# K turned in 32 by 32 squares on VectorE instead of on TensorE, in a decode block of cached attention and a gated MLP

## The chip, the cores and the metric

The kernel runs on one core of one Trainium2 chip. The metric is the device time of one execution in microseconds. A profiled execution also gives a span, which is about 1.8 us shorter than its time. Runs are called fast or slow: here a run is slow when it lies over 1.5% above the fastest run of the same kernel. All ratios use fast runs.

Engine names in the profile: PE is TensorE, PEld its weight loads, DVE is VectorE, ACT is ScalarE, POOL is GpSimd, SP issues the DMAs. PEclk is the clock that TensorE was granted; in the text, *warm* is the full clock and *cold* is half of it: the profile's windows over one PV of the changed kernel show a granted clock of 1.00 where its products took 1.90 us and of 0.50 where they took 3.59.

## The reference, cut to what matters

```python
# x: 1x1x640; 32 heads of 128; caches 1x32x4096x128; MLP 640 -> 1728 -> 640; all bf16
h  = x + A(layernorm(x))            # A: one query against 4096 cached keys and values, then wo
q  = (x @ wq).reshape(..., 32, 128)
p  = softmax(einsum("bhqd,bhkd->bhqk", q, k_cache) * 128 ** -0.5)
A  = einsum("bhqk,bhkd->bhqd", p, v_cache).reshape(..., 4096) @ wo
h2 = h + (gelu(hn @ w_gate) * (hn @ w_up)) @ w_down      # hn = layernorm(h)
```

Each cached key and value is used once. The two caches are 67 MB of the 84 MB that the kernel reads.

## The kernel before

Four heads are one *quad*. A quad's K is one tile of 128 partitions by 128 rows by 128 columns (4 MB); its V has the same shape. The score products of this kernel contract over partitions, so K has to be turned before them. The kernel before does this with 128 products per quad against an identity matrix; VectorE and ScalarE copy the turned K from PSUM back to SBUF. K and V have two buffers each.

```python
def pe_transposes(slot, mark, after):
    ...
    for g in range(NG):                       # 16 groups of 8 products of 128 x 128
        ...
        for b in range(GRP):
            inst = PE.transpose(tp_b[g % NBANK][:, b * DH : (b + 1) * DH], kt[slot][:, g * GRP + b, :], ident[:])
...
def pe_scores(slot, half, ready, mark):       # 128 products with 4 columns
    ...
        inst = PE.matmul(s_ps[half][:, j % (NB // 2), :], lhsT=kt[slot][:, j, :],
                         rhs=q8[:, slot * QH : (slot + 1) * QH], start=True, stop=True)
...
def pe_pv(slot, half, mark):                  # 128 products with 4 columns
    ...
        inst = PE.matmul(o_ps, lhsT=vt[slot][:, j, :], rhs=e_t[:, j, :], start=(j == 0), stop=(j == NB - 1))
...
with nc.Fori(0, TURNS, engines=(only_pe,), head_slot={only_pe: HEAD}):   # two quads a turn
...
for m in range(NQ):                           # the order of the loads, on one queue
    load_k(m)                                 # waits for the scores of quad m-2; the last K in two halves
    if m in (0, 2, 4):
        load_wo(m // 2)
    ...
    load_v(m)                                 # waits for PV of quad m-2
load_wo(TURNS - 1)
load("wg", ...); load("wu", ...)              # then the four pieces of w_down
```

The softmax here doesn't subtract the row's maximum and nothing guards it: scores larger than these inputs give would overflow.

Of the kernel before, what the change touches and what calls it, by code (L numbers as in the profile page):

```python
# [9 lines left out]
def kernel(  # L10
# [13 lines left out]
    nc = tc.nc  # L24
    bf16 = mybir.dt.bfloat16
# [18 lines left out]
    GRP = 8  # L44
    NG = NB // GRP
    YR = 4
    YW = D // YR
    TURNS = NQ // SLOTS
    HG = QH * SLOTS
    NBANK = 4  # L50
    HEAD = 0
    ON_ACT = (1, 4, 6, 9, 11, 14)
# [22 lines left out]
    big = sb("big", [P, 2 * SLOTS * TILE + 2 * W_MLP], bf16)  # L75
# [4 lines left out]
    def tile_at(i):  # L80
        return part(i * TILE, TILE).rearrange("p (j d) -> p j d", d=DH)

    kt = [tile_at(i) for i in range(SLOTS)]
    vt = [tile_at(SLOTS + i) for i in range(SLOTS)]
    wq_sb = part((2 * SLOTS - 1) * TILE, DC * NH * DH).rearrange("p (c n) -> p c n", c=DC)
    wg_sb = part(2 * SLOTS * TILE, W_MLP).rearrange("p (c f) -> p c f", c=DC)
    wu_sb = part(2 * SLOTS * TILE + W_MLP, W_MLP).rearrange("p (c f) -> p c f", c=DC)
# [14 lines left out]
    q_row = sb("q_row", [P, 2, 4 * DH], bf16)  # L102
    q_sb = sb("q_sb", [P, NH], bf16)
    q8 = sb("q8", [P, HG], bf16)
    e_t = sb("ex", [P, NB, QH], bf16)
    rs_all = sb("rs_all", [P, 2, NH])
    rs_cur = sb("rs_cur", [P, HG])
    rinv = sb("rinv", [P, HG])
    o_raw = sb("o_raw", [P, NH])
# [24 lines left out]
    tp = [bank(f"tp{i}") for i in range(NBANK)]  # L134
    tp_b = [t.bitcast(bf16) for t in tp]
    tp_g = [t[:].rearrange("p (b d) -> p b d", d=DH) for t in tp_b]
    s_bank = [bank(f"s{h}") for h in "ab"]
    o_bank, a_bank = bank("o"), bank("a")
    s_ps = [t[:, 0 : QH * NB // 2].rearrange("p (j i) -> p j i", i=QH) for t in s_bank]
    attn_ps = a_bank[:, 0:YW]  # L140
    qr_ps = s_bank
    q_ps = tp_b[0]
    o_ps = o_bank[:, 0:QH]

    def small(b):
        return b[:, 16 : 16 + 2 * DC], b[:, 32 : 32 + HG], b[:, 48 : 48 + HG]

    (m_ps, t_ps, r_ps), (m_end, t_end, r_end) = small(o_bank), small(tp[3])
    g_ps, u_ps, y_ps = tp[0][:, 0 : RG + LAST], tp[1][:, 0 : RG + LAST], tp[2][:, 0:YW]

    names = (
        [f"{t}{i}{h}" for t in "kv" for i in range(SLOTS) for h in "ab"]
        + ["x", "wq", "wo", "wo_in", "wg", "wu", "wd0", "wd1", "wd2", "wd3", "out"]
        + ["pe", "dve", "act", "pool", "q", "dve_pe", "act_pe", "y", "all"]
# [39 lines left out]
    for ps in (attn_ps, qr_ps[0][:], qr_ps[1][:]):  # L194
        dve(lambda: DVE.memset(ps, 0.0), False)
    dve(lambda: DVE.memset(rs_all[:], 0.0), False)
    DVE_RS = dve(lambda: DVE.memset(rs_cur[:], 1.0), False)
    dve(lambda: DVE.memset(ones_f[:], 1.0), False)
    POOL_IDENT, POOL_E, POOL_COPIED = 2, 3, 6
    DVE.wait_ge(S["pool"], POOL_IDENT)  # L200
    by_c = ident[:].rearrange("p (c j) -> p c j", j=HG)
    with nc.allow_low_precision(reason="sums of one 1 and zeros"):
        dve(lambda: DVE.reduce_sum(row_of[:], by_c, AX.X), False)
        dve(lambda: DVE.reduce_sum(col_of[:], by_c.rearrange("p c j -> p j c"), AX.X), False)

# [33 lines left out]
    DVE_Q = DVE_XN + 2  # L239

    def group(slot, g):
        return kt[slot][:, g * GRP : (g + 1) * GRP, :]

    def pe_transposes(slot, mark, after):
        ready = [("act_pe", EA_T[slot][g]) if g in ON_ACT else ("dve_pe", EV_T[slot][g]) for g in range(NG)]
        for g in range(NG):
            if g % (NG // 2) == 0:
                landed(f"k{slot}{'ab'[g // (NG // 2)]}")
            if g >= NBANK:
                PE.wait_ge(S[ready[g - NBANK][0]], ready[g - NBANK][1])  # L250
            for b in range(GRP):
                inst = PE.transpose(  # L252
                    tp_b[g % NBANK][:, b * DH : (b + 1) * DH], kt[slot][:, g * GRP + b, :], ident[:]
                )
            mark(("T", g), inst)
            if g in after:
                after[g]()
        return ready[-NBANK:]

    def pe_scores(slot, half, ready, mark):  # L260
        for j in range(half * NB // 2, (half + 1) * NB // 2):
            g, b = divmod(j, GRP)
            if b == 0 and g >= NG - NBANK:
                PE.wait_ge(S[ready[g - NG + NBANK][0]], ready[g - NG + NBANK][1])
            inst = PE.matmul(  # L265
                s_ps[half][:, j % (NB // 2), :],
                lhsT=kt[slot][:, j, :],
                rhs=q8[:, slot * QH : (slot + 1) * QH],
                start=True,
                stop=True,  # L270
            )
        mark(("s", half), inst)

    def pe_pv(slot, half, mark):
        landed(f"v{slot}{'ab'[half]}")
        PE.wait_ge(S["act_pe"], EA_EXP[slot][half])
        for j in range(half * NB // 2, (half + 1) * NB // 2):
            inst = PE.matmul(  # L278
                o_ps, lhsT=vt[slot][:, j, :], rhs=e_t[:, j, :], start=(j == 0), stop=(j == NB - 1)
            )  # L280
            if j == NB // 2:
                mark("pv first", inst)
        mark("pv", inst)

    def pe_project(w, mark, last):
        for j in range(HG):
            for r in range(YR):
                inst = PE.matmul(  # L288
                    attn_ps[32 * r : 32 * r + 1, :],
                    lhsT=o_row[:, j : j + 1],  # L290
                    rhs=w[:, j, r * YW : (r + 1) * YW],
                    start=False,
                    stop=last and j == HG - 1,
                    skip_group_check=True,
                    tile_position=(0, 32 * r),
                )
        mark("project", inst)
# [21 lines left out]
    ON_DVE = [g for g in range(NG) if g not in ON_ACT]  # L319
    SPREAD_AT, ROW_AT = 3, 6  # L320
    EV_Q, EV_RS = 1, 3
    EV_T = [{}, {}]
    n = EV_RS
    for i, g in enumerate(ON_DVE):
        if i == SPREAD_AT:
            n += 1
            EV_SPREAD = n
        if i == ROW_AT:
            n += 1
            EV_ROW = n  # L330
        n += 1
        EV_T[0][g] = n
    n += 1
    for g in ON_DVE:
        n += 1
        EV_T[1][g] = n
    EV_ALL = n
    EA_T, EA_EXP = [{}, {}], [[], []]
    n = 0
    for slot in range(SLOTS):  # L340
        for g in ON_ACT:
            n += 1
            EA_T[slot][g] = n
        EA_EXP[slot] = [n + 1, n + 2]
        n += 2
    EA_ALL = n

    start = mark_at("start")
    PE.wait_ge(S["dve"], DVE_XS)
    pe_moments(m_ps, x_col, start)  # L350

    def pe_queries():
        PE.wait_ge(S["dve"], DVE_XN)
        for c in range(DC):
            if c == 0:
                landed_once("wq")
            for b in range(2):
                for r in range(4):
                    h = 16 * b + 4 * r
# [3 lines left out]
                        rhs=wq_sb[:, c, h * DH : (h + 4) * DH],  # L363
# [6 lines left out]
        PE.wait_ge(S["pool"], POOL_IDENT)  # L370
        PE.wait_ge(S["act"], 1)
        PE.wait_ge(S["dve"], DVE_Q - 1)
        for b in range(2):
            for i in range(4):
                k = (4 * b + i) * P
                inst = PE.transpose(q_ps[:, k : k + P], q_row[:, b, i * DH : (i + 1) * DH], ident[:])
        inst.then_inc(S["q"], 1)

    pe_queries()
    PE.wait_ge(S["dve"], DVE_Q)  # L380
    PE.wait_ge(S["pool"], POOL_COPIED)

    base = done["pe"]
    only_pe = mybir.EngineType.PE
    with nc.Fori(0, TURNS, engines=(only_pe,), head_slot={only_pe: HEAD}):
        for slot in range(SLOTS):
            mark = mark_at(slot)
            after = {}
            if slot == 0:

                def totals():
                    PE.wait_ge(S["dve_pe"], EV_RS)
                    pe_totals(t_ps, mark)

                def reorder():
                    PE.wait_ge(S["dve_pe"], EV_SPREAD)
                    pe_reorder(r_ps, mark)

                after = {ON_DVE[SPREAD_AT - 1]: totals, 8: reorder}
            ready = pe_transposes(slot, mark, after)  # L400
            if slot == 0:
                PE.wait_ge(S["dve_pe"], EV_ROW)
                PE.wait_ge(S["wo"], 1)
                PE.sem_inc(S["wo"], -1)
                pe_project(wo_t, mark, False)
            for half in range(2):
                pe_scores(slot, half, ready, mark)
            for half in range(2):
                pe_pv(slot, half, mark)
        PE.sem_inc(S["dve_pe"], -EV_ALL)  # L410
        PE.sem_inc(S["act_pe"], -EA_ALL)
# [95 lines left out]
    def load_kv(which, m, tiles, src, free):  # L507
        slot = m % SLOTS
        if m >= SLOTS:
            SP.wait_ge(S["pe"], free)  # L510
# [216 lines left out]
```

## Time and profile before

| | before |
|---|---|
| time, median of 6 runs | 206.97 us (206.08 to 207.66) |
| span of the profiled run | 204.8 us |
| busy: PE, DVE, ACT | 145.5, 73.4, 81.4 us |
| DMA | 84.4 MB, share 0.99 to 1.01 from 20 to 180 us |
| first product of the MLP | 192.72 us |

The page of the kernel before. The first lines give busy time, share of the span and instructions of each engine; the other two are the DMA's busy share and rate in 40 equal slices, where a 9 is 90% or more.

```profile
...
PE 145.5 (71%) x3409; PEld 135.7 (66%) x3409; DVE 73.4 (36%) x185; ACT 81.4 (40%) x179; POOL 19.2 (9%) x17
...
DMA  7999999999999999999999999999999999999990
GB/s 248 408 458 416 396 475 406 437 432 451 406 419 416 441 426 448 435 429 410 435 448 398 447 455 416 422 435 448 429 429 416 416 429 461 429 401 432 400 350 32
...
```

No engine is busy all the time, but the DMA is, from the second slice to the last but one. The windows of the same run say it with numbers; the last three columns are the granted clock, the DMA's share and its rate.

```profile
...
100.00:120.00 20.00, 16.44 (x388) 16.21 (x386) 7.64 (x17) 9.92 (x22) 0.00 (x0) 0.74 1.00 429
...
199.00:201.00 2.00, 1.60 (x44) 1.09 (x48) 0.22 (x2) 0.00 (x0) 0.00 (x0) 0.50 0.43 163
201.00:203.00 2.00, 0.76 (x20) 0.31 (x20) 0.33 (x2) 0.00 (x0) 0.00 (x0) 0.50 0.00 0
...
```

The DMA ends in the window from 199 to 201 us. What is left after it is a short tail. Two lines of the chain of waits (start, duration, what; the span is that of the profiled run) mark the last quad: the first of its products with the identity, and the product that follows its PV.

```profile
...
170.75 0.87 PE tp_103 L252 x8
...
187.15 0.54 PE tp_106 L300 x2
...
```

The last quad's K is turned from 170.75 on, and its PV product ends at 187.15. The timeline of TensorE shows the rest. The columns are start, duration, engine, line, operation, output and inputs, number, and in brackets the idle time before it and what ended that.

```profile
...
192.72 2.16 PE L454 MATMUL tp_103<-big,hc 128*1 128x416 bf16 x25 [0.53 <-DVE hc L664]
196.09 2.16 PE L454 MATMUL tp_104<-big,hc 128*1 128x416 bf16 x25 [1.22 <-DMA big<-in_B_w_up_dram]
199.40 2.36 PE L437 MATMUL tp_105<-big,hid 128*1 128x160 bf16 x60 [1.15 <-DVE hid L680]
```

The MLP begins at 192.72. The up product (196.09) waits for its weights from the DMA, and the down product (199.40) takes 2.36 us. It waits for `hid`, which VectorE writes from both products:

```profile
...
199.07 0.18 DVE L680 TENSOR_TENSOR hid<-g_sb,u_col 128x15 bf16<-128x15 f32 x1
...
```

### The profile page before, as it was taken

To read this page: it belongs to the slowest core of one execution; us is meant where nothing else is said; L and a number is where in the kernel's file an instruction comes from. 1 tells how busy PE (TensorE), PEld (TensorE's weight loads), DVE (VectorE), ACT (ScalarE), POOL (GpSimd) and SP (SyncE) were. 2 spreads that over 40 slices of the span, in tenths; PEclk is the share of its full clock that TensorE was granted. 3 is DMA by queue.
4 is the path that set the end of the run, shared out by engine and by line. 5 is a ranking of instruction groups with operands and counts; after the bars stand their busy time and mean duration, and the time that the engine had idled before them with its cause. 6 is when DMAs were issued, how large, how long until landed. Compare 5 with 4: busy or idle time off the path is not lost. (4 is left out here: it accounts for less than half of the span.)

```text
span 204.8 us, 7384 instructions
## 1 busy us (share of the span) xinstructions
PE 145.5 (71%) x3409; PEld 135.7 (66%) x3409; DVE 73.4 (36%) x185; ACT 81.4 (40%) x179; POOL 19.2 (9%) x17
## 2 busy tenths in 40 slices
PE   0001769935997399849984998299839989986654
PEld 0000269935997399849974997299739979986322
DVE  4006126500570058005701660047006702832570
ACT  0000234533377047704670557037704671771000
POOL 8300000340000001700000026000000000000000
PEclk9999967975797579757975797579757975995555
DMA  7999999999999999999999999999999999999990
GB/s 248 408 458 416 396 475 406 437 432 451 406 419 416 441 426 448 435 429 410 435 448 398 447 455 416 422 435 448 429 429 416 416 429 461 429 401 432 400 350 32
DMA packets 3963, 84.39 MB, mean 412 GB/s; under 512 B 464, under 2 KB 464, under 8 KB 752
## 3 DMA queue, kind: packets, MB, share of 16 engines
q1 hardware_dynamic: 3952, 84.23, 96.7%
q8 instruction: 8, 0.13, 0.3%
q14 instruction: 3, 0.02, 0.0%
HBM read 84.23 MB, written 0.00 MB: 411 GB/s over the span
## 5 line engine op out<-in xcount | busy, mean ns | idle before, releaser
L278 PE MATMUL o<-ex,big 128*128 128x4 bf16 x1024 | 29.9, 166 | 10.6 <-ACT ex L567 6.4
L278 PEld LDWEIGHTS o<-ex,big 128*128 128x128 bf16 x1024 | 28.5, 103 | 11.9 <-ACT ex L567 7.6
L553 ACT COPY big<-tp_104 128x1024 bf16<-128x1024 bf16 x16 | 16.2, 1012 | 49.6 <-PE tp_104 L252 49.6
L252 PE MATMUL tp_103<-ident,big 128*128 128x128 bf16 x256 | 23.7, 247 | 13.5 <-PEq L176 13.5
L252 PEld LDWEIGHTS tp_103<-ident,big 128*128 128x128 bf16 x256 | 19.2, 114 | 13.9 <-issue 13.9
L580 DVE COPY big<-tp_103 128x1024 bf16<-128x1024 bf16 x24 | 16.5, 688 | 21.1 <-PE tp_103 L252 21.1
L252 PE MATMUL tp_104<-ident,big 128*128 128x128 bf16 x256 | 23.6, 246 | 0.0
L252 PE MATMUL tp_105<-ident,big 128*128 128x128 bf16 x256 | 23.3, 244 | 0.0
L500 POOL COPY wo<-wo_in 128x5120 bf16<-128x5120 bf16 x3 | 13.4, 4451 | 105.8 <-PE a L288 105.8
L252 PE MATMUL tp_106<-ident,big 128*128 128x128 bf16 x256 | 22.0, 235 | 0.0
L252 PEld LDWEIGHTS tp_104<-ident,big 128*128 128x128 bf16 x256 | 19.3, 113 | 0.0
L252 PEld LDWEIGHTS tp_105<-ident,big 128*128 128x128 bf16 x256 | 19.2, 112 | 0.0
L252 PEld LDWEIGHTS tp_106<-ident,big 128*128 128x128 bf16 x256 | 18.1, 108 | 0.0
L265 PE MATMUL sb<-q_77,big 128*128 128x4 bf16 x512 | 14.3, 164 | 4.8 <-issue 4.8
L580 DVE COPY big<-tp_106 128x1024 bf16<-128x1024 bf16 x24 | 16.6, 690 | 2.6 <-PE tp_106 L252 2.2
L553 ACT COPY big<-tp_105 128x1024 bf16<-128x1024 bf16 x16 | 16.2, 1014 | 2.9 <-PE tp_105 L252 2.9
L265 PEld LDWEIGHTS sb<-q_77,big 128*128 128x128 bf16 x512 | 13.6, 96 | 4.9 <-issue 4.9
L567 ACT ACTIVATE ex<-sa 32x64 bf16<-32x64 f32 x32 | 9.8, 307 | 11.4 <-PE sa L265 11.2
L580 DVE COPY big<-tp_105 128x1024 bf16<-128x1024 bf16 x16 | 11.1, 691 | 8.4 <-PE tp_105 L252 8.1
L265 PE MATMUL sa<-q_77,big 128*128 128x4 bf16 x512 | 14.0, 164 | 0.0
L265 PEld LDWEIGHTS sa<-q_77,big 128*128 128x128 bf16 x512 | 13.5, 96 | 0.6
L637 DVE COPY o_raw<-o 128x4 f32<-128x4 f32 x4 | 0.7, 163 | 36.4 <-PE o L278 36.4
(111 smaller groups left out, 112.2 us busy)
## 6 DMA issues: line engine op xcount, KB each, us to landing
big<-in_A_v_cache_dram SPq DMA_DIRECT2D x8, 4096.0 KB, 33.9
big<-in_A_k_cache_dram SPq DMA_DIRECT2D x7, 4096.0 KB, 26.6
big<-in_A_wq_dram SPq DMA_DIRECT2D x1, 5120.0 KB, 15.5
wo_in<-in_A_wo_dram SPq DMA_DIRECT2D x4, 1280.0 KB, 27.4
big<-in_A_k_cache_dram SPq DMA_DIRECT2D x2, 2048.0 KB, 24.4
big<-in_B_w_gate_dram SPq DMA_DIRECT2D x1, 2160.0 KB, 39.5
big<-in_B_w_up_dram SPq DMA_DIRECT2D x1, 2160.0 KB, 44.9
big<-in_B_w_down_dram SPq DMA_DIRECT2D x1, 1280.0 KB, 32.7
```

Source lines behind the costliest of these rows:

```text
L252: inst = PE.transpose(tp_b[g % NBANK][:, b * DH : (b + 1) * DH], kt[slot][:, g * GRP + b, :], ident[:])
L265: inst = PE.matmul(s_ps[half][:, j % (NB // 2), :], lhsT=kt[slot][:, j, :], rhs=q8[:, slot * QH : (slot + 1) * QH], start=True, stop=True,)
L278: inst = PE.matmul(o_ps, lhsT=vt[slot][:, j, :], rhs=e_t[:, j, :], start=(j == 0), stop=(j == NB - 1))
L500: POOL.tensor_copy(wo_t[:], wo_in[:]).then_inc(S["wo"], 1)
L553: ACT.copy(group(m % SLOTS, g), tp_g[g % NBANK]).then_inc(S["act_pe"], 1)
L567: inst = ACT.activation(e_t[r, cols, i], s_ps[half][r, :, i], AF.Exp, scale=SCALE, accum_out=rs_all[r, half, h : h + 1])
L580: DVE.tensor_copy(group(m % SLOTS, g), tp_g[g % NBANK]).then_inc(S["dve_pe"], 1)
L637: event(DVE.tensor_copy(o_raw[:, HG * turn : HG * turn + QH], o_ps))
```

## The change

The intent is to free TensorE and ScalarE from turning and copying. VectorE turns K from SBUF to SBUF in squares of 32 by 32, on pairs of bf16 that it takes for one fp32. Scores and PV then have the long side in the free dimension: 32 products of 512 columns per quad in place of 128 of 4 columns. The queries stand in a wide, mostly zero matrix so that each chunk's scores fall into its own row of one PSUM bank. One quad is one turn of TensorE's loop, and the loop starts with a turn that skips its body. V keeps one buffer only, and the last K is no longer loaded in halves.

```diff
-    def pe_transposes(slot, mark, after):            # 128 products and 16 copies a quad: gone
+    def pe_scores(mark):
+        for c in range(NC):
+            PE.wait_ge(S["kt"], c + 1)
+            for k in range(2):
+                for e in range(2):
...
+                    inst = PE.matmul(
+                        s_bank[:],
+                        lhsT=q_wide[:, 2 * k + e, NC - 1 - c : NC - 1 - c + P],
+                        rhs=kt_at[:, k, c, :, e],
...
+    def pe_pv(mark):
...
+                inst = PE.matmul(
+                    pv_bank[32 * r : 32 * r + VG * QH, :],
+                    lhsT=e_t[:, j : j + VG, :].rearrange("p j h -> p (j h)"),
+                    rhs=vt[:, j : j + VG, :].rearrange("p j d -> p (j d)"),
...
+                    tile_position=(0, 32 * r),
...
+    def pe_outputs(mark):                             # 4 fp32 products pick each head's own rows
...
-    with nc.Fori(0, TURNS, engines=(only_pe,), head_slot={only_pe: HEAD}):
+    with nc.Fori(0, NQ + 1, engines=only_pe) as turn:
+        with PE.If(turn == 1):
...
+        with PE.If(turn > 0):
...
+            pe_scores(mark)
+            PE.wait_ge(S["act_pe"], 1)
+            pe_totals(t_ps, mark)
+            landed("v")
+            pe_pv(mark)
+            PE.wait_ge(S["act_pe"], 2)
+            pe_outputs(mark)
+            PE.wait_ge(S["dve_pe"], 1)
+            pe_reorder(r_ps, mark)
...
+            pe_project(mark)
...
     for m in range(NQ):
         load_k(m)
-        if m in (0, 2, 4):
+        if m % 2 == 0:
             load_wo(m // 2)
...
         load_v(m)                                     # now waits for PV of quad m-1
-    load_wo(TURNS - 1)
...
+    for m in range(NQ):                               # VectorE, in order
...
+        DVE.wait_ge(S[f"k{m % SLOTS}"], 16)
...
+        for c in range(NC):
+            DVE.transpose(to[:, c], of[:, c].rearrange("p (j k n) -> p j k n", k=2, n=HP)).then_inc(S["kt"], 1)
+        wait_pe(pe_at(m, "s"))
+        assert dve(lambda: DVE.transpose(s_turned[:].rearrange("p j c -> p (j c)"), s_bank[:]), False) == D_SCORES[m]
...
+        wait_pe(pe_at(m, "o"))
+        dve(lambda: DVE.tensor_tensor(o_col[:, own], o_ps, rinv[:], op=ALU.mult))
...
+        spread().then_inc(S["dve_pe"], 1)
+        wait_pe(pe_at(m, "reorder"))
+        DVE.tensor_copy(o_row[:], r_ps).then_inc(S["dve_pe"], 1)
```

## The prediction

> What bounds the kernel now: the DMA. Windows of 20 us from 20 to 160 show a DMA share of 0.99 to 1.01 at 425 to 436 GB/s; 84.2 MB leave the queue about 199.5 us into a span of 204.8. Compute only has to keep up, plus a tail: first MLP matmul at 192.7, end 204.8, so 12.1 us from there (rstd chain, gelu chain, down product, store). The change moves the same bytes in nearly the same order, so it cannot win more than 1 or 2 us. The question is whether the new compute chain keeps pace. A quad costs the DMA 9.04 MB / 0.429 = 21.1 us.
>
> Removed: 1024 PE transposes, 64 PSUM evacuations (DVE 690 ns, ACT 1013 ns), 1024 score and 1024 PV matmuls with 128-column weights. Their busy time was hidden. Also lost: the second V buffer, the split last K, and the overlap of one quad's transposes with the finish of the previous one: VectorE now turns K and also serves the small steps, so a quad is one serial chain.
>
> That chain, from K landed (estimates from trace durations):
> - 8 VectorE transposes of 1024 fp32. The trace has 416 elements in 612 ns and 64 in 207 ns (PSUM source), so about 1.15 ns each plus 140 ns.[...] 160 elements read at 20-byte steps took 464 ns[...]. I take 1.18 us each: 9.4.
> - Scores follow chunk by chunk, 512 wide: the query products show 0.43 us cold and 0.21 warm. Cold for some 4 us, then catching up; 1.2 us after the last transpose.
> - Turning the scores 0.7.
> - 4 exps of 128 elements at a wide step: 64 elements took 307 + 200 ns; about 0.65 each: 2.6.
> - Totals 0.5; PV in four column tiles, 8 x 0.43 cold (PE idle 3.7 us before): 3.6. ScalarE copy 0.65.
> - Four fp32 output matmuls, eight passes of 0.17 to 0.27: 1.8.
> - o_col, spread, reorder, o_row: 1.0, next query 0.2.
> Sum about 21.7 us, against 21.1 of DMA: compute chain and DMA almost level, the chain slightly longer. The first quad starts at about 28.5 (queries at 24.4, q turned, three memsets), the last near 28.5 + 7 x 21.4 = 178; its K cannot land before about 174.4. The last quad takes about 21.7 + 1.3 (projection) + 2.2 to the MLP, + 12.1: 37.3. Span about 214 to 216; the timed run was 1.7 above the span. So 216 us. Were the chain 1.5 us per quad shorter, the DMA would set the pace, and only the tail would be longer: 210. 3 us longer: about 235.
>
> What would show it: DMA share falls under 0.97 with gaps in front of V loads; the SP queue waits on the PV product; VectorE busy about 110 us, PE clearly below half of its 145; STREAM_TRANSPOSE of 1024 near 1.2 us; the chain of waits alternates VectorE, PE, ScalarE; first MLP matmul near 202 instead of 192.7. The skipped turn: no "issue" gaps on PE in the first quad, where the trace before has 1.4 to 3.4 us each; worth little.
>
> Wrong if: the score products with a two-element step in their moving operand run at half rate, or the PE never warms (slower, 235 and more); transposes take 2 ns per element (much slower, 270); exps and PV run faster and the PE stays warm, so that DMA binds (209 to 211, same). Chances: faster 0.02, same 0.24, slower 0.74. Range 209 to 229.

The sum came to 21.65 us, the "about 21.7" above: the 1.18 us of a transpose are 1024 times the 1.15 ns of the trace, without the 140 ns (with them it would have been 1.32).

## The result, and the profile after

| | before | after |
|---|---|---|
| time, median | 206.77 us (20 runs) | 210.61 us (10 runs, 209.18 to 215.5; the highest is slow) |
| span of the profiled run | 204.8 us | 207.6 us |
| busy: PE, DVE, ACT | 145.5, 73.4, 81.4 us | 126.3, 102.6, 23.0 us |
| instructions | 7384 | 2520 |
| last quad begins, first MLP product | 170.75, 192.72 us | 175.14, 196.72 us |

The ratio of the fast runs is 1.017, with a 95% interval of 1.0141 to 1.02. A ratio is the mean time of one kernel's fast runs over that of the other's fast runs of the same rounds, so it is not quite the ratio of the medians above. A later set of runs on the same chip as an experiment gave 1.0204 (1.0162 to 1.0246) for the same kernel. The change makes the kernel 1.7 to 2.0% slower, clear of noise. I had predicted 4.4%.

The page of the changed kernel, the same lines as before:

```profile
...
PE 126.3 (61%) x1002; PEld 57.9 (28%) x1010; DVE 102.6 (49%) x192; ACT 23.0 (11%) x75; POOL 19.2 (9%) x16
...
DMA  7999999999999999999989999999999999999930
GB/s 245 445 412 404 424 434 486 423 404 448 437 417 397 461 410 480 417 417 442 448 384 474 417 410 475 410 429 417 422 437 454 429 417 436 436 400 426 369 142 3
...
```

ScalarE lost 58 us of work and TensorE over two thirds of its instructions, yet the DMA's row looks as before. The windows agree: the DMA's share is still 1.00, and it ends in the same two microseconds.

```profile
...
100.00:120.00 20.00, 15.23 (x107) 7.25 (x107) 10.94 (x16) 2.62 (x9) 4.49 (x2) 0.74 1.00 429
...
199.00:201.00 2.00, 1.88 (x22) 0.72 (x17) 1.72 (x8) 0.07 (x1) 0.00 (x0) 0.50 0.19 67
...
```

So the serial chain that I had feared does not hold the DMA back. The groups of the changed kernel show the slack: after the count stand busy time and mean duration of one in ns, then the idle time in front and what ended it.

```profile
...
L247 PE MATMUL s<-big,q_wide 128*128 128x512 bf16 x248 | 73.1, 454 | 19.0 <-DVE big L540 18.8
L540 DVE STREAM_TRANSPOSE big<-big 128x1024 f32<-128x1024 f32 x64 | 73.0, 1207 | 9.4 <-DVEq L536 9.4
...
```

The transposes took 1207 ns each, close to my 1.18 us, and VectorE waited 9.4 us in front of them. That wait is for a landed K (the semaphore wait at L536 is the one on the K load). Five of the eight quads begin with it. The score products wait 19.0 us for VectorE in their turn, which is the pace of the transposes. Two neighbours in the timeline of VectorE:

```profile
...
129.08 0.17 DVE L551 CAST o_row<-o 128x8 bf16<-128x8 f32 x1 [0.27 <-PE o L301]
...
133.20 9.13 DVE L540 STREAM_TRANSPOSE big<-big 128x1024 f32<-128x1024 f32 x8 [3.81 <-DVEq L536]
...
173.21 0.17 DVE L551 CAST o_row<-o 128x8 bf16<-128x8 f32 x1 [0.27 <-PE o L301]
...
175.14 9.13 DVE L540 STREAM_TRANSPOSE big<-big 128x1024 f32<-128x1024 f32 x8 [1.62 <-DVEq L536]
...
```

VectorE has written o_row of one quad at 129.25 and could turn the next K, but that K lands at 133.2 only. The same happens before the last quad. From first transpose to o_row, the first seven chains take 18.5, 18.3, 21.5, 19.7, 18.2, 21.7 and 18.4 us: 19.5 on average, where I had summed 21.7.

Part of that is the clock. PV, 32 products in four column tiles, took 1.90 us in five quads, 2.72 in one and 3.59 in two. The three lines below stand for one of each; the granted clock in these stretches was 1.00, 0.50 and 0.67:

```profile
...
63.04 1.90 PE L262 MATMUL pv<-big,ex 128*16 128x512 bf16 x32
...
83.16 3.59 PE L262 MATMUL pv<-big,ex 128*16 128x512 bf16 x32
...
104.75 2.72 PE L262 MATMUL pv<-big,ex 128*16 128x512 bf16 x32
...
```

The tail of the changed kernel, on TensorE:

```profile
...
189.08 1.90 PE L262 MATMUL pv<-big,ex 128*16 128x512 bf16 x32
...
196.72 2.10 PE L396 MATMUL g<-big,hc 128*1 128x416 bf16 x24 [0.53 <-DVE hc L564]
...
203.25 1.41 PE L379 MATMUL y<-big,hid 128*1 128x160 bf16 x60 [2.37 <-DVE hid L580]
```

and on VectorE, the last step in front of the down product:

```profile
...
203.01 0.18 DVE L580 TENSOR_TENSOR hid<-g_sb,u_col 128x15 bf16<-128x15 f32 x1
...
```

Take the pieces of the two spans. The last quad begins 4.4 us later (175.14 against 170.75). From there to the end of PV it takes 15.8 us (16.4 before). From there to the MLP it takes 5.7 us (5.6 before). From the first MLP product to the end of the span it takes 10.9 us (12.1 before). The sum is 4.4 - 0.6 + 0.1 - 1.2 = 2.8 us, rounding aside, which is the difference of the spans. The MLP won its 1.2 us almost wholly because the down product ran warm (1.41 us against 2.36). The up product no longer waited for its weights, but that gained next to nothing: from the first MLP product to the end of `hid` it takes 6.5 us in both kernels (196.72 to 203.19 after, 192.72 to 199.25 before). Nor is the warm product a sure gain of the change: in the fast profiles of e5 and e12 below, after the same wait of 2.4 us for `hid`, it ran cold again (2.36 and 2.37 us); what decides this is not shown. The profiled run of the changed kernel took 209.43 us, which is 2.9 above its partner (206.54), while the medians are 3.8 apart.

The last quad begins later because it has to wait for its whole K; TensorE before was held by the PV of the quad in front instead, which ends at 170.75. Part of it may be the order of the loads: the last block of wo (1280 KB) stands in front of the last K in the changed kernel and behind the last V in the old one. At 429 GB/s that is 3.1 us of DMA, an estimate; it was not tried separately, because the projection of the quad in front needs this block.

### The profile page after: what moved, and what is told of

Its sections match the earlier page's. It is cut to its first block, busy times and chain, and to the rows that moved or that the text cites. A ratio compares the mean times of both kernels' runs of the same rounds, so it can differ in the third digit from the quotient of the medians.

```text
span 207.6 us, 2520 instructions
## 1 busy us (share of the span) xinstructions
PE 126.3 (61%) x1002; PEld 57.9 (28%) x1010; DVE 102.6 (49%) x192; ACT 23.0 (11%) x75; POOL 19.2 (9%) x16
## 5 line engine op out<-in xcount | busy, mean ns | idle before, releaser
L247 PE MATMUL s<-big,q_wide 128*128 128x512 bf16 x248 | 73.1, 454 | 19.0 <-DVE big L540 18.8
L540 DVE STREAM_TRANSPOSE big<-big 128x1024 f32<-128x1024 f32 x64 | 73.0, 1207 | 9.4 <-DVEq L536 9.4
L247 PEld LDWEIGHTS s<-big,q_wide 128*128 128x128 bf16 x256 | 27.6, 111 | 63.1 <-DVE big L540 24.0
L490 ACT ACTIVATE ex<-s_turned 32x128 bf16<-32x128 f32 x32 | 15.6, 487 | 121.2 <-DVE o_col L543 120.9
L262 PE MATMUL pv<-big,ex 128*16 128x512 bf16 x256 | 19.4, 456 | 0.0
L274 PE MATMUL o<-of_row,pv_sb 128*128 128x4 f32 x64 | 10.9, 293 | 5.5 <-ACT pv_sb L499 5.5
L274 PEld LDWEIGHTS o<-of_row,pv_sb 128*128 128x128 f32 x64 | 10.2, 242 | 10.8 <-ACT pv_sb L499 10.8
L286 PE MATMUL a<-wo,o_row 128*1 128x160 bf16 x256 | 7.8, 281 | 2.1 <-DVE o_row L551 2.1
L262 PEld LDWEIGHTS pv<-big,ex 128*16 128x16 bf16 x256 | 6.4, 99 | 7.9 <-issue 3.9
L490 ACT ACTIVATION_READ_ACCUMULATOR ex<-s_turned 32x1 f32 x32 | 5.9, 184 | 0.0
```

The source lines that it names most:

```text
L247: inst = PE.matmul(s_bank[:], lhsT=q_wide[:, 2 * k + e, NC - 1 - c : NC - 1 - c + P], rhs=kt_at[:, k, c, :, e], start=first, stop=last,)
L262: inst = PE.matmul(pv_bank[32 * r : 32 * r + VG * QH, :], lhsT=e_t[:, j : j + VG, :].rearrange("p j h -> p (j h)"), rhs=vt[:, j : j + VG, ...
L274: inst = PE.matmul(o_ps, lhsT=pv_sb[:, i * DH : (i + 1) * DH], rhs=of_row[:, i * QH : (i + 1) * QH], start=i == 0, stop=i == VG - 1,)
L286: inst = PE.matmul(attn_ps[32 * r : 32 * r + 1, :], lhsT=o_row[:, j : j + 1], rhs=wo_t[:, j, r * YW : (r + 1) * YW], start=False, stop=j = ...
L490: inst = ACT.activation(e_t[r, :, i].rearrange("p (c j) -> p c j", c=NC), s_turned[r, :, 0:NC].rearrange("p j c -> p c j"), AF.Exp, scale= ...
L540: DVE.transpose(to[:, c], of[:, c].rearrange("p (j k n) -> p j k n", k=2, n=HP)).then_inc(S["kt"], 1)
```

## The experiments

The theory after the result: **A**, the DMA sets the pace for seven quads, and only the way from the last K to the end shows in the time. The rival is my prediction: **B**, the serial chain of each quad sets the pace. The experiments insert idle work in different places, keep the clock up, and then shorten the tail. All results were correct.

### Idle work behind each of the first seven quads

```diff
+    def idled():
+        wait(DVE, "idle", len(n_idle))
+        DVE.transpose(idle[:], q_turned[:]).then_inc(S["idle"], 1)
+        n_idle.append(1)
...
         DVE.tensor_copy(o_row[:], r_ps).then_inc(S["dve_pe"], 1)
+        if m < NQ - 1:
+            for _ in range(1):       # e2_every_4: range(4)
+                idled()
```

> One idle VectorE transpose (128x512 fp32, about 0.72 us plus 0.03) is put behind each of the first seven quads, 5.2 us in all. Theory A (the DMA sets the pace; the seven chains sum to 137 us in the trace against 146.6 us between the start of the first and of the last quad, so 9.5 us of slack): last quad starts where it did, near 175; time within 0.7 us of the changed kernel, 210 to 211.5. Theory B (as I predicted: the serial chain sets the pace): 5.2 us more, near 216.

Measured: fast runs 210.35, 211.65 and 212.28 us, ratio 1.0212 (1.0149 to 1.0275). That is the changed kernel's own ratio in its second set, 1.0204; two of the three times lie just above the 210 to 211.5 that I gave. In the profile the last quad begins at 175.77 instead of 175.14:

```profile
...
175.77 9.12 DVE L548 STREAM_TRANSPOSE big<-big 128x1024 f32<-128x1024 f32 x8
...
L548 DVE STREAM_TRANSPOSE big<-big 128x1024 f32<-128x1024 f32 x64 | 73.0, 1208 | 4.3 <-DVEq L544 4.2
...
```

VectorE's wait for K fell from 9.4 to 4.2 us, by just the 5.2 us of work put in, and the last quad now begins without a wait. B would have needed 5.2 us, 2.5%, on top of the time. So A: the seven chains have slack.

> Four idle transposes (3.0 us) behind each of the first seven quads, 21 us in all. Theory A: the first 9.5 us vanish in the slack, 11 to 12 us show: about 222; the DMA share falls under 0.97 in the middle of the run. Theory B: all 21 us show: about 231. A theory in which only the tail counts: no change.

Measured: two fast runs of 224.02 and 223.91 us, two slow ones (228.86 and 235.82); ratio 1.0818. Of 21 us inserted, some 13 show against the changed kernel (224.0 less 210.6). A had 222 and B had 231: the slack is there and is finite, about 8 us by this measure and 9.4 by the wait in the profile.

### Idle work in the last quad alone

```diff
         wait_pe(pe_at(m, "o"))
+        if m == NQ - 1:
+            for _ in range(4):
+                idled()
```

> Four idle transposes (3.0 us) in the last quad alone, between the output product and o_col. Theory A: after the last K has landed all is one serial chain to the end, so all 3.0 us show: 213 to 214, although the same work behind all the other quads together costs nothing. If the end were set by the last MLP weights (DMA done near 199.5), less than 1 us would show.

Measured: two fast runs of 213.59 and 216.54 us, ratio 1.0388 (1.0292 to 1.0484). Against 1.017 to 1.0204 that is 1.8 to 2.2%, or 3.8 to 4.5 us, for 3.0 us of work. The interval is wide and includes 3.0. What it rules out is that the work vanishes. By these means, 3 us in the last quad cost 3.8 to 4.5, and 5.2 us spread over the other seven (e1) cost 0.2 to 0.9.

### Keeping TensorE busy while it waits for the exps

```diff
         PE.sem_inc(S["kt"], -NC)
         mark("s", inst)
+        for _ in range(8):
+            PE.matmul(t_bank[:, 16:512], lhsT=ident[:],
+                      rhs=q_turned[:].bitcast(bf16)[:, 0:496], start=True, stop=True)
```

> Eight products without use (128x496, into an unused part of a PSUM bank) follow the scores of each quad, where PE waits 2.9 us for the exps. Theory: PV takes 3.6 us in the quads where the clock fell in that wait and 1.9 where it did not; kept busy, PE stays warm: PV 1.9 and output products 1.05 us in all eight quads (now five of eight and six of eight), the sum of seven chains falls from 137 to about 130 us, and the time moves only through the last quad and the steadier tail: 209 to 210.3, 0.3 to 1.5 us less than the changed kernel's median. Rival: the clock follows something else (the time since the last K landed, or load of other engines), PV stays at 3.6 in some quads.

The PV products in the timeline of this run, in the two quads that were cold or half cold above:

```profile
...
83.06 1.90 PE L270 MATMUL pv<-big,ex 128*16 128x512 bf16 x32
...
104.71 1.90 PE L270 MATMUL pv<-big,ex 128*16 128x512 bf16 x32
...
```

PV took 1.90 us in all eight quads, and the output products 1.05 (in the changed kernel these are five quads of eight, not the six that I wrote above). So my 3.6 us for PV was the cold figure, and filling the wait of 2.9 us in front of PV took the cold away. Why the same wait left PE warm in five quads and not in the three others is not shown. The time, however, did not move: 210.65 us, ratio 1.0174 (1.012 to 1.0229). I had expected 0.3 to 1.5 us less. Shorter chains only lengthen the waits for K: 15.5 us in all, against 9.4, and 4.3 in front of the last quad, against 1.6, which begins at 175.11 as before.

```profile
...
L548 DVE STREAM_TRANSPOSE big<-big 128x1024 f32<-128x1024 f32 x64 | 73.0, 1208 | 15.6 <-DVEq L544 15.5
...
```

### The last K in two halves

```diff
-        load(f"k{m % SLOTS}", kr[m % SLOTS], rows_of(A_k_cache, m))
+        if m == NQ - 1:
+            w = TILE // 2
+            for i in range(2):
+                load(f"kl{i}", kr[m % SLOTS][:, i * w : (i + 1) * w], rows_of(A_k_cache, m)[:, i * w : (i + 1) * w])
+        else:
+            load(f"k{m % SLOTS}", kr[m % SLOTS], rows_of(A_k_cache, m))
```

> The last K load is cut in two halves with a semaphore each; VectorE, free at 173.4 in the trace of the changed kernel while the whole K landed at 175.1, starts on the first half. Theory (DMA sets the pace until the last K, then a serial tail): the last quad starts 1.5 to 1.7 us earlier and the end comes 1.5 us earlier: 209.0, or 1.009 to 1.012 of before. Rival (the end is set by the last MLP weights or by the chain of all quads): no change, 210.6.

Measured: 209.72 us, ratio 1.0136 (1.0098 to 1.0173), so 0.3 to 0.7% (0.7 to 1.4 us) less than the changed kernel's two sets: a gain of the expected sign and of half of the expected 1.5 us to nearly all of it, but not clear of noise, since the intervals overlap. In the profile the last quad begins at 172.93 (2.2 us earlier) and its scores end 2.7 us earlier, but its PV took 3.26 us and the down product 2.36. Those 2.3 us, compared with 1.90 and 1.41, are the clock.

### Without the skipped turn

```diff
-    with nc.Fori(0, NQ + 1, engines=only_pe) as turn:
-        with PE.If(turn == 1):
-            PE.wait_ge(S["dve"], DVE_XS)
...
+    PE.wait_ge(S["dve"], DVE_XS)
...
+    with nc.Fori(0, NQ, engines=only_pe):
```

> The loop loses its first, skipped turn: the start code stands in front of the loop, as in the kernel before, and the loop makes eight turns. Expected from the trace before: gaps of PE put down to issue in the first turn, 1.4 to 3.4 us each, together up to 9 us in two quads; here fewer instructions per quad, so 2 to 5 us in the first quad. If the DMA sets the pace with 9.5 us of slack, the time hardly moves: 210.5 to 212.5, unless the first PV ends after the second K has landed (47.5), which delays the second V. If the serial chain set the pace, all 2 to 5 us would show: 213 to 216.

Measured: fast runs 209.42, 209.54 and 210.82 us, ratio 1.0135 (1.0092 to 1.0177). The skipped turn gains nothing that these runs can see; the fast runs lie about 1 us under the range that I gave, which stays unexplained. The profiled run was a slow one, but in it no gap of 0.5 us or more between TensorE's products is put down to issue, and its weight loads wait for issue 0.3 us at most, so there was nothing for the skipped turn to hide. The kernel before has four such gaps of 1.4 to 3.4 us, 9.0 us together, in a loop body of two quads with far more instructions (7384 in the whole kernel, against 2520).

### Shortening the tail

The last K in four loads, and its first two chunks turned in the wait of the quad before (e7); the same with the useless products (e8); with V in two halves as well (e9); with the three memsets moved out of the way of the first quad (e10).

```diff
+        if m == NQ - 2:              # e7
+            query(NQ - 1)
+            turn_chunks(NQ - 1, range(2))
         wait_pe(pe_at(m, "o"))
...
-        load("v", vt.rearrange("p j d -> p (j d)"), rows_of(A_v_cache, m))
+        for i, name in enumerate(("va", "vb")):       # e9; PV waits for vb in front of its second half
+            cols = slice(i * TILE // 2, (i + 1) * TILE // 2)
+            load(name, vt.rearrange("p j d -> p (j d)")[:, cols], rows_of(A_v_cache, m)[:, cols])
```

> The last K comes in four loads, and its first two chunks are turned before o_col of the quad before it, where VectorE waits for PV and the output products. Theory (serial tail after the last K): scores of the last quad end about 3.5 to 4 us earlier (182 instead of 185.8), the MLP starts near 193, the end is 3 to 4 us earlier: 206.5 to 207.5, level with the kernel before. If the tail is not what costs, 210.6.

Measured: 208.82 us, ratio 1.009 (1.0061 to 1.0119): better than the changed kernel, short of the expectation. TensorE was cold in part of the profiled run: the PV in front of the last quad took 3.59 us, and the last scores ended at 185.6, hardly earlier than before.

> The same with the eight useless products behind the scores, so that PE is warm when the last quad's scores start. Theory: without them the last scores are paced by a cold PE (0.43 us a product for some 3 us); with them by VectorE: 0.5 to 1 us less than the run without, 205.7 to 206.8, slightly better than the kernel before. Rival: as the useless products alone changed nothing in the time, no difference here either.

Measured: 207.5 us, ratio 1.0018 (0.9981 to 1.0054). Warmth, worth nothing alone in e4, is worth 0.7% once the last quad no longer waits for the whole K (e7 and e8 ran in the same rounds, and their intervals do not overlap). The gain over e7 came, 1.3 us in the medians; the time that I had expected, 205.7 to 206.8, did not, since e7 itself had come out higher. In its profile the last scores end at 181.6, 4.3 us earlier than in the changed kernel, and the last PV waits 1.0 us for its V:

```profile
...
173.25 8.31 PE L248 MATMUL s<-big,q_wide 128*128 128x512 bf16 x31
...
185.86 3.38 PE L271 MATMUL pv<-big,ex 128*16 128x512 bf16 x32 [1.01 <-PEq L170]
...
```

> On top of the early chunks and the useless products, every V load is cut in two halves, and PV starts on the first. In the run before this one the last PV waited 1.0 us for the last V (landed 185.86) and then ran cold, 3.4 us. Theory (what is left of the tail is the way from the last V to the end): PV ends 1.5 to 2.2 us earlier, the time 1 to 2 us: 205.5 to 206.5, 0.992 to 0.997 of before. Rival (the last MLP weights, DMA done near 200, set the end): 207.3, no change.

Measured: 207.47 us, ratio 1.0051 (1.0019 to 1.0084). No gain; the rival was right. The MLP now starts at 192.97, and its up and down products wait for the DMA:

```profile
...
192.97 2.16 PE L406 MATMUL g<-big,hc 128*1 128x416 bf16 x25 [0.53 <-DVE hc L599]
196.23 2.16 PE L406 MATMUL u<-big,hc 128*1 128x416 bf16 x25 [1.10 <-DMA big<-in_B_w_up_dram]
199.89 2.36 PE L389 MATMUL y<-big,hid 128*1 128x160 bf16 x60 [1.50 <-DMA big<-in_B_w_down_dram]
```

> The same, and the three memsets (1.1 us) in front of the first quad are moved into its wait for the output products. If the DMA sets the pace, a first quad that starts 1.1 us earlier changes the median by less than 0.3 us, but its first PV ends before the second K has landed in more of the runs, so the highest times come down.

Measured: 207.27 us (207.06 to 207.52), ratio 1.0024 (0.9999 to 1.0049). The median hardly moves and the highest time falls from 208.68 to 207.52, both as expected of A, though in six runs each.

### V halves alone, memsets alone

> V halves alone on the changed kernel. There the last PV starts 3 us after the last V has landed (189.1 against about 185), so V is not waited for: no change, 1.015 to 1.019 of before. If halves made the DMA itself faster or the V buffer come free earlier, it would show here.

Measured: 211.08 us, ratio 1.0211 (1.0182 to 1.024). No gain, as expected, though the ratio lies just above the range that I gave.

> Only the three memsets moved, on the changed kernel: the chain of all seven quads starts 1.1 us earlier. Theory DMA: median unchanged within 0.5 us (1.013 to 1.018 of before), fewer runs above 211. Theory chain: 1.1 us less, 1.012.

Measured: fast runs 209.78, 211.66 and 211.7 us, slow ones of 213.79, 214.24 and 214.46; ratio 1.019 (1.0136 to 1.0245). The ratio does not move beyond the changed kernel's own two (1.017 and 1.0204), though it lies just above the range that I gave. The expected effect on the high times failed: there were more of them here, not fewer.

### Filling the last waits, and the changed kernel again

```diff
     end("g", up(g_ps, wg_sb, {0: "wg"}))
+    for _ in range(2): ...           # the same useless product as in e4
     end("u", up(u_ps, wu_sb, {0: "wu"}))
+    for _ in range(4): ...
```

> On top of the version with everything: two useless products between g and u and four between u and y of the MLP, where PE waits for the last weights at half clock. Theory (with the tail shortened, the DMA's end sets the time, then a down product that runs cold, 2.36 us, where the changed kernel's took 1.41 warm): y near 1.4 to 1.8 us, the time 0.5 to 0.9 us less, 206.4 to 206.8, 0.997 to 1.000 of before. Rival: PE stays at half clock or the products delay u and y: no change or 0.5 us more.

Measured: 207.05 us (206.84 to 207.16), ratio 1.0018 (0.9995 to 1.0041). The down product became warm in parts, but it waits for the last weights twice:

```profile
...
200.00 1.40 PE L389 MATMUL y<-big,hid 128*1 128x160 bf16 x52 [0.22 <-DMA big<-in_B_w_down_dram]
201.81 0.31 PE L389 MATMUL y<-big,hid 128*1 128x160 bf16 x8 [0.41 <-DMA big<-in_B_w_down_dram]
```

It ends at 202.1, where the cold one of e9 ended at 202.3. So the end of the DMA sets the time of this version, and the 0.5 to 0.9 us that I had expected did not come. In the kernel before, the last bytes come before 201, and the cold down product runs on to 201.8. No version here beats the kernel before; the best ones tie with it.

> The changed kernel itself once more, on the same chip as the run beside it, as a measure of its spread: 1.014 to 1.020 of before, 209.2 to 212, perhaps one run above.

Measured: fast runs 209.32 to 212.23 us and a slow one of 215.3; ratio 1.0204 (1.0162 to 1.0246), just above what I had expected. The profile caught the slow run. Its two windows around the second V load show where this run lost time:

```profile
...
40.00:45.00 5.00, 2.10 (x19) 1.02 (x22) 0.92 (x3) 2.02 (x8) 0.00 (x0) 0.78 1.02 439
45.00:50.00 5.00, 4.09 (x32) 2.23 (x24) 0.16 (x1) 0.58 (x1) 0.00 (x0) 0.50 0.67 229
...
```

The first PV was cold (3.59 us), so it ended at 47.2; only then is the second V load issued (V has one buffer), and the DMA had run dry: a share of 0.67 in that window. In the fast profile of the changed kernel the share there is 0.98. This tells of slow runs alone and is not used for the difference between the kernels. That all slow runs have this cause is not shown. The record does hint at it: of the 54 timed runs of the changed kernel and its variants without the useless products 11 were slow, of the 28 with them none, and of the 60 of the kernel before none. The variants differ in other ways too.

## Why the prediction was wrong

The direction (slower) and the time (inside 209 to 229, near the lower edge) held, but the direction partly by luck: I had put a chain that outlasts the DMA first, and the loss comes from the last K and the tail alone. The size did not hold: I forecast 4.4% and 1.7 to 2.0% came.

- **DMA bound, cannot win more than 1 or 2 us:** right. The DMA's share stayed at 1.00, and even e13, with its tail cut to the DMA's end, only ties.
- **"Sum about 21.7 us, against 21.1 of DMA: compute chain and DMA almost level, the chain slightly longer":** this step failed. The seven chains took 19.5 us on average, less than the 21.1 of DMA, so the DMA set the pace. PV was mis-sized most: 3.6 us estimated, 1.90 in five quads of eight and 2.5 on average over the seven chains. To count its 32 products as eight was right: cold they took 3.59. I had put the wait in front of it at 3.7 us and taken it for granted that it costs the warm clock; the wait was 2.9 us and cost it in two quads, and in part in a third. The exps took 2.1 us and not 2.6 (start to start 0.52 us: 487 ns each, with the accumulator's read of 184 ns overlapping), and the output products 1.05 us warm and not 1.8 (1.87 in the three other quads; their four products are eight records each time). The transposes (9.13 against 9.4) and the turning of the scores (0.72 against 0.7) were sized well; the scores ended 1.5 us after the last transpose on average and not 1.2. The "some 4 us" cold are seen in the second quad: the granted clock was 0.50 from 50.65, 0.75 from 54 to 55 and 1.00 after that.
- **The first quad near 28.5, "the last near 28.5 + 7 x 21.4 = 178":** measured 28.54 and 175.14. The last K's landing set it, which I had put at 174.4. What the chains in between took did not matter within their slack: e1 added 5.2 us to them for less than 1.
- **The tail, 37.3 us from the last K:** measured 32.5. The chain of the last quad to o_row took 18.6 and not 21.7, for the reasons above; from there to the MLP it took 3.0 and not 3.5; the MLP took 10.9 and not 12.1, because the figure that I had copied from the trace before holds a cold down product. These 4.8 us and the 2.9 us of the line above are the whole error of the span.
- **The alternative, "the DMA would set the pace, and only the tail would be longer: 210":** this is what happened, and I gave it too little weight.
- **VectorE busy about 110 us:** 102.6. **PE "clearly below half of its 145":** wrong, 126.3. The score products alone are busy for 73.1 us in the profile, 454 ns each, and I had not added them up. **64 PSUM evacuations:** a slip without effect, there are 128 (16 a quad).
- **"DMA share falls under 0.97":** it did not (0.99 to 1.02 from 20 to 180 us). **First MLP product near 202:** 196.72. **The queue waits on PV:** it did, but with loads still ahead of it, so nothing was lost.
- **Not half rate for a moving operand with a two-element step, and not 2 ns per element for the transposes:** both right. In the second quad the records of single score products last 610 to 628 ns while the granted clock was 0.50 (up to 53.8) and 385 to 388 ns while it was 1.00 (from 55.2); the 512-column query products, whose operand is packed, last 0.59 to 0.64 us and, at the end of their burst, 0.38 to 0.39. The granted clock reads 1.00 for this whole burst, so that the longer ones were cold is read from their length alone. A transpose of 1024 elements took 1207 ns, 1.18 ns per element. Eight in a row without waits took 9.13 us, 1.14 each, so 66 ns of each are hidden behind its neighbour.

## What to carry to other kernels

Here the DMA was busy all the time, and work taken off the engines gained nothing. What remains to be asked is how long the kernel runs after the last bytes it has to wait for, and which load stands in front of them in the queue. The serial chain per quad cost nothing while it was shorter than the quad's transfer (19.5 against 21.1 us, and e1); beyond the slack most of it showed (e2). Size a burst of products after a wait of about 3 us both warm and cold, because in this kernel both occur, 1.90 and 3.59 us for the same PV: of eight waits of 2.9 us two left PV cold and a third left it partly cold (2.72 us), while eight useless products in the wait kept all eight at 1.90 (e4).
